# Diagonal spreads on GpSimd, state scaling on ScalarE, and unit 8's k turned through HBM, in a fused recurrence and MLP kernel

## The chip, the core and the metric

The kernel runs on one core of one Trainium2 chip. The metric is device time in microseconds (us) of one execution. Five engines run side by side, each through its own instructions in order: TensorE (PE), VectorE (DVE), ScalarE (ACT), GpSimd (POOL) and SyncE (SP, which only issues transfers here). Each waits on semaphores for what the others make.

## The reference

A linear recurrence over 768 time steps for 4 batches and 8 heads of 48 channels, and behind it a two-layer MLP with an ELU between (384 to 2048 to 384), all in float32:

```python
for t in range(S):
    cur = np.einsum('bhd,bhe->bhde', u[None] * kt, vt)
    y[:, :, t] = np.einsum('bhd,bhde->bhe', rt, state + cur)
    state = wt[:, :, :, None] * state + np.einsum('bhd,bhe->bhde', kt, vt)
...
h = x @ w_in
g = np.where(h > 0.0, h, alpha * (np.exp(np.minimum(h, 0.0)) - 1.0))
return (g @ w_out).astype(np.float32)
```

## The kernel before

**The recurrence in units.** The sequence is worked on in 24 units. Units 0 to 3 ("whole") are one batch each with 128 steps; units 4 to 23 hold two batches with 64 steps each. In a unit the recurrence is turned into products of matrices. Two scans on VectorE (es, L461, and gs, L471) make running products of the decay w; rh (L476) multiplies k and r by them. TensorE forms the scores of all pairs of steps in PSUM (task s: four transposes of k, L563, then score products, L570). A tile `ams` receives the diagonal (each step's own term, r times u times k summed over a head's channels, called md, spread over a matrix that is zero elsewhere: task sp) and then, by a predicated copy from PSUM on VectorE (mk, L599 to L605), the part above it. Task v multiplies `ams` with the values (L550) and updates the state (L640). Between units the state is scaled by the unit's total decay (sc, L632) and added to (up, L698).

**md** comes, in units 0 to 3, from VectorE (rkc, r times k, L495), TensorE (pd, L500) and a copy on ScalarE (L504); from unit 4 on from three VectorE steps (rk, rku, md). **sp** is run for units 0 to 7 by ScalarE, as eight scaled copies of the identity (L518), and for units 8 to 23 by GpSimd, as two selects on 64 partitions (L529).

**From unit 8 on** (`STACK`) r and the state are copied by DMA beside the scores and the values (rc, L540, and tc, L546), and the scores of the next unit are made one unit ahead (va). k with time on the partitions comes for units 9 to 21 (`TURN`) from a 32 by 32 transpose on VectorE (tn, L618), four transfers to HBM (tw, L623) and one back (tk, L627); for the others from transposes on TensorE (tr) and a copy on ScalarE (kt, L609).

**The MLP.** Each group of four units gives 512 columns, and 16 blocks of 128 hidden channels are run over them. float32 is split into a high and a low part (fp32r), so that g1 (`ph`, L267) and g2 (`acc`, L298) are nine matmuls each. Between them stand r1 and r2 on ScalarE (L271, L274), stt on VectorE (L277, written back to `m`), gh on ScalarE (L281) and gl on VectorE (L285). `ph` has two buffers, so a g1 waits for the stt of the g1 two before it. The weights are made at the start from raw words: a (ScalarE, L231), cc (VectorE, L235), wh (ScalarE, and for two blocks GpSimd, L727), wl (VectorE, L731).

**What sets the order.** The order on every engine is written out by hand as a table of names (`SEQUENCE`), one row per engine; a name is a task and its number, such as `sp.4`. `FILL` puts matmuls on a tile of ones (L426) ahead of named TensorE tasks before the first g2; they compute nothing that is used. One such float32 matmul shows as two records in the trace. Transfers are issued in order on SP's queue, and tiles with a fixed number of buffers (`SLOTS`) make a task wait for the last use of its buffer.

## Time and profile before

| | us |
|---|---|
| median of 3 runs (484.72 to 485.08) | 484.99 |
| the profiled execution | 486.13 |
| its span, first to last instruction | 484.4 |
| TensorE busy | 475.7 |
| VectorE busy | 359.1 |
| ScalarE busy | 260.4 |
| GpSimd busy | 40.7 |

The span is what the profile shows. The profiled execution took 1.73 us more than its span, and 1.14 us more than the median of the runs without a profile. Matmuls overlap in the engine and their ends are modelled, so the time that a matmul costs is read from one start to the next. The granted TensorE clock is 1.00 in every stretch of the trace.

### The profile page before, as it was taken

Reading aid. Unit: us, or ns where it says so; the run is one execution under the profiler, and the core shown is the slowest. Engines: PE = TensorE matmul, PEld = TensorE weight load, DVE = VectorE, ACT = ScalarE, POOL = GpSimd, SP = SyncE. Lnnn points to the kernel's source line nnn. Section 1 sums busy time; section 2 is a strip of 40 time slices with the busy share of each in tenths; the row PEclk is TensorE's granted clock in tenths of the full one; section 3 lists DMA queues with packets and bytes.
Section 4 is the critical chain, followed back from the end, with each engine's and each line's share of the span. In section 5 each row is a group of like instructions: output and inputs, shape, how many; then the busy total and the mean of one; then the engine's idle time right before and its main releaser. Section 6 shows DMA issues by size and latency. Waiting matters only on the chain.

```text
span 484.4 us, 12143 instructions
## 1 busy us (share of the span) xinstructions
PE 475.7 (98%) x4978; PEld 395.3 (82%) x4978; DVE 359.1 (74%) x545; ACT 260.4 (54%) x535; POOL 40.7 (8%) x56
## 2 busy tenths in 40 slices
PE   9999999999999999999999999999999999999996
PEld 8888888878888787788788878888888888888885
DVE  7999999999899999979997896655426453333332
ACT  4998878856544443635343643536544343644442
POOL 3000000004011302012101101101001000000000
PEclk9999999999999999999999999999999999999999
DMA  8999477417485664855754747332521100100001
GB/s 276 363 319 293 149 250 244 146 41 205 89 260 129 187 141 117 241 146 104 209 156 107 216 101 207 89 87 81 133 59 39 38 2 1 65 2 0 0 2 66
DMA packets 75418, 64.91 MB, mean 134 GB/s; under 512 B 56976, under 2 KB 57360, under 8 KB 75360
## 3 DMA queue, kind: packets, MB, share of 16 engines
q1 hardware_dynamic: 74784, 63.33, 46.3%
q8 instruction: 39, 0.64, 0.6%
q10 hardware_dynamic: 576, 0.79, 0.5%
q14 instruction: 19, 0.16, 0.1%
HBM read 49.67 MB, written 8.13 MB: 119 GB/s over the span
## 4 chain that ended last, share of the span: by engine, by line
PE 75%; DVE 16%; issue 3%; DMA 3%; ACT 2%; DVEq 0%; POOL 0%; POOLq 0%
PE ph L267 32%; PE acc L298 31%; PE py L550 2%; PE px L570 2%; PE acc L426 2%; DVE ams L605 2%; DVE m L277 2%; PE px L550 2%; DVE gl L285 2%; DVE eg L461 2%; DMA w<-in_wkr_dram 1%; DVE k L476 1%; PE px L640 1%; DVE tops L734 1%; DMA k<-in_wkr_dram 1%
## 5 line engine op out<-in xcount | busy, mean ns | idle before, releaser
L271 ACT ACTIVATE m<-ph 128x512 f32<-128x512 f32 (+2 forms) x103 | 58.3, 567 | 102.0 <-PE ph L267 69.8
L267 PE MATMUL ph<-xh,w_l 128*128 128x512 f32 (+1 forms) x294 | 112.0, 381 | 0.0
L298 PE MATMUL acc<-gh,w_l 128*128 128x512 f32 (+1 forms) x292 | 111.2, 381 | 0.0
L277 DVE SCALAR_TENSOR_TENSOR m<-m,ph 128x512 f32<-128x512 f32 (+2 forms) x103 | 66.2, 646 | 57.2 <-ACT m L274 56.6
L281 ACT CAST gh<-m 128x512 fp32r<-128x512 f32 (+1 forms) x98 | 58.9, 602 | 86.6 <-PE acc L298 60.4
L267 PE MATMUL ph<-xh,w_h 128*128 128x512 f32 (+1 forms) x264 | 102.5, 388 | 1.8 <-DVE m L277 1.4
L298 PE MATMUL acc<-gh,w_h 128*128 128x512 f32 (+1 forms) x264 | 102.3, 388 | 0.0
L285 DVE TENSOR_TENSOR gl<-m,gh 128x512 fp32r<-128x512 f32 (+1 forms) x98 | 67.0, 690 | 46.3 <-ACT gh L281 45.1
L298 PE MATMUL acc<-gl,w_h 128*128 128x512 f32 (+1 forms) x264 | 100.4, 380 | 0.3 <-DVE gl L285 0.3
L267 PE MATMUL ph<-xl,w_h 128*128 128x512 f32 (+1 forms) x264 | 100.3, 380 | 0.0
L267 PEld LDWEIGHTS ph<-xh,w_l 128*128 128x128 f32 x294 | 55.3, 188 | 10.8
L298 PEld LDWEIGHTS acc<-gh,w_l 128*128 128x128 f32 x292 | 54.9, 188 | 10.5
L274 ACT ACTIVATE m<-m 128x512 f32<-128x512 f32 (+2 forms) x103 | 61.2, 601 | 1.7
L267 PEld LDWEIGHTS ph<-xh,w_h 128*128 128x128 f32 x264 | 49.6, 188 | 13.8 <-DVE m L277 3.3
L298 PEld LDWEIGHTS acc<-gh,w_h 128*128 128x128 f32 x264 | 49.6, 188 | 10.3
L298 PEld LDWEIGHTS acc<-gl,w_h 128*128 128x128 f32 x264 | 49.6, 188 | 9.7 <-DVE gl L285 0.7
L267 PEld LDWEIGHTS ph<-xl,w_h 128*128 128x128 f32 x264 | 49.7, 188 | 8.9
L529 POOL TENSOR_SCALAR_AFFINE_SELECT ams<-md 64x512 f32<-64x512 f32 x32 | 32.1, 1002 | 242.2 <-PE py L550 164.2
L461 DVE TENSOR_TENSOR_SCAN eg<-w,reset 112x520 f32<-112x520 f32 (+1 forms) x24 | 30.1, 1256 | 2.8 <-DMA w<-in_wkr_dram 2.8
L471 DVE TENSOR_TENSOR_SCAN eg<-w,reset 112x520 f32<-112x520 f32 (+1 forms) x24 | 30.3, 1263 | 0.8
L476 DVE TENSOR_TENSOR k<-k,eg 112x1024 f32<-112x1024 f32 x24 | 29.1, 1214 | 0.1
L605 DVE COPY_PREDICATED ams<-upper_h,px 64x512 f32<-64x512 uint32 x32 | 23.5, 735 | 1.4 <-PE px L570 0.9
(127 smaller groups left out, 501.6 us busy)
## 6 DMA issues: line engine op xcount, KB each, us to landing
wraw<-in_wraw_dram SPq DMA_DIRECT2D x16, 767.8 KB, 6.6
rk<-in_rk_dram SPq DMA_DIRECT2D x20, 384.0 KB, 4.5
k<-in_wkr_dram SPq DMA_DIRECT2D x13, 512.0 KB, 4.3
w<-in_wkr_dram SPq DMA_DIRECT2D x24, 227.9 KB, 4.1
k<-in_wkr_dram SPq DMA_DIRECT2D x11, 448.0 KB, 5.5
wide<-in_vp_dram SPq DMA_DIRECT2D x32, 128.0 KB, 4.0
out_dram<-o SPq DMA_DIRECT2D x15, 256.0 KB, 4.0
rows<-turn SPq DMA_DIRECT2D x52, 64.0 KB, 2.8
```

Of the source, the lines that this page charges most:

```text
L267: nc.tensor.matmul(ph, w[f][:, 0, k], y[:, k], start=(k == n == 0), stop=(k == NK - 1 and n == 2))
L271: act(s["m"], s["ph"], AF.Relu, scale=-1.0)
L274: act(s["m"], s["m"], AF.Exp, scale=-1.0)
L277: stt_(s["m"], s["m"], -1.0, s["ph"], ALU.add, ALU.max)
L281: nc.scalar.copy(s["gh"], s["m"])
L285: nc.vector.tensor_tensor(s["gl"], s["m"], s["gh"].bitcast(F32), ALU.subtract)
L298: nc.tensor.matmul(a_, w[f][:, 1, m], fold(s, g[:, a:b]), start=(first and n == 0), stop=(final and n == 2))
L461: nc.vector.tensor_tensor_scan(out=eg[:, 0, 0:n][:, ::-1], data0=u_["w"][:, 1:n + 1][:, ::-1], data1=reset[:, 0, 0:n][:, ::-1], initial=0. ...
L471: nc.vector.tensor_tensor_scan(out=u_["eg"][:, 1, 1:n + 1], data0=u_["w"][:, 0:n], data1=reset[:, 1, 0:n], initial=0.0, op0=ALU.mult, op1= ...
L476: tt(t, t, u_["eg"][:, :, 0:u_["n"]].rearrange("d z (s t) -> d z s t", t=u_["L"] + 1)[..., 1:], ALU.mult)
L529: nc.gpsimd.affine_select(out=am[rs, h].rearrange("t q p s -> t (q p) s"), in_=u_["md"][rs].rearrange("t q p -> t (q p)").unsqueeze(2).bro ...
L605: nc.vector.copy_predicated(u_["am"][rs, h], above[L][rs], pa[rs])
```

## The change

Four things change, and with them the whole order.

- **Spreads.** sp of units 0 to 7 goes from ScalarE to GpSimd (`spread_rows`): one select of 128 partitions by 1024 elements for units 0 to 3, two of 64 by 512 for units 4 to 7.
- **Scaling.** sc of units 4 to 11 goes from one VectorE instruction to eight scaled copies on ScalarE (`scale_state_act`), each of 112 partitions by 48 elements. Units 12 to 23 stay.
- **Unit 8's k** is turned as that of units 9 to 21: tn.8 on VectorE, tw.8 and tk.8 through HBM. tr.8 on TensorE and kt.8 on ScalarE go.
- **pd** writes in the order that md is read in, at two places of its bank by turns, behind the place of the transposes; it no longer waits for the bank.
- **Sequences and fillers** are new for all engines. The fillers before the first g2 are 45 instead of 36.

```diff
-FILL = {("pd",0):17,("s",0):5,("pd",1):3,("s",1):2,("v",1):8,("s",2):1,("g2",0):0}
+FILL = {("s",0):23,("s",1):5,("v",0):2,("g1",0):4,("v",1):7,("g1",1):4,("g2",0):0}
...
-SPREAD = ["ACT"] * 8 + ["POOL"] * 16
+SPREAD = ['ROWS'] * 8 + ['POOL'] * 16
+SCALE = ['ACT' if i < 12 else 'DVE' for i in range(NU)]
-TURN = range(9, 22)
+TURN = range(8, 22)
...
     PE="""
-pd.0 s.0 pd.1 v.0 s.1 g1.0 pd.2 v.1 g1.1 g1.2 s.2 g2.0 g2.1 g1.3 pd.3 g2.2 v.2 g1.4 s.3 g2.3 g1.5 v.3 g1.6 g1.7 g2.4 g1.8 g2.5 g2.6 g1.9 g2.7 g2.8
+s.0 pd.0 pd.1 s.1 v.0 g1.0 v.1 g1.1 g1.2 g2.0 g2.1 pd.2 s.2 g1.3 g1.4 v.2 pd.3 g2.2 s.3 g2.3 g1.5 v.3 g1.6 g2.4 g1.7 g1.8 g2.5 g2.6 g1.9 g2.7 g1.10
...
     POOL="""
-const reset.4 clear.0 clear.1 clear.2 sp.9 sp.8 sp.10 sp.11 sp.12 wh.1 wh.0 sp.13 sp.14 sp.15 sp.16 sp.17 sp.18 sp.19 sp.20 sp.21 sp.22 sp.23
+const sp.0 sp.1 sp.2 reset.4 sp.3 clear.0 sp.4 sp.5 sp.6 clear.1 sp.7 sp.8 clear.2 sp.9 wh.1 sp.10 wh.0 sp.11 sp.12 sp.13 sp.14 sp.15 sp.16 sp.17
+sp.18 sp.19 sp.20 sp.21 sp.22 sp.23
...
     def diag_pe(u_):
-        u_["pd"] = pd = single()[:, 0:NS].rearrange("t (p z) -> t p z", p=NP)
+        lo = NP * R2 + NS * (u_["i"] % 2)
+        u_["pd"] = pd = single()[:, lo:lo + NS].rearrange("t (z p) -> t z p", p=NP)
         for p in range(NP):
-            nc.tensor.matmul(pd[:, p], u_["rkc"][:, p, :], ubd[:, p, :], start=True, stop=True)
+            nc.tensor.matmul(pd[:, :, p], u_["rkc"][:, p, :], ubd[:, p, :], start=True, stop=True)
...
-    def spread_act(u_):
-        am = diagonal(u_)
-        for q in range(2):
-            for p in range(NP):
-                act(am[:, q, p], ident if u_["whole"] else ident_h, AF.Copy, scale=u_["md"][:, q, p:p + 1])
...
+    def spread_rows(u_):
+        am, n = diagonal(u_).rearrange("t q p s -> t (q p) s"), u_["L"]
+        for lo in range(0, C, n):
+            rs = slice(lo, lo + n)
+            nc.gpsimd.affine_select(out=am[rs], in_=u_["md"][rs].rearrange("t q p -> t (q p)").unsqueeze(2).broadcast_to([n, NS, n]),
+                                    pattern=[[0, NS], [1, n]], compare_op=ALU.is_equal, fill=0.0, base=0, channel_multiplier=-1)
...
+    def scale_state_act(u_):
+        lo = u_["b"].start
+        for p in range(NP):
+            for h in range(2):
+                act(sv[:, lo + h, p], sv[:, lo + h, p], AF.Copy, scale=u_["pc"][:, 2 * p + h])
...
-            add(("s", i), "PE", K["s0" if u_["whole"] else "s8" if new else "s"], lambda u_=u_: score(u_),
-                [("rh", i), ("const",)] + [("sp", i)] * (i > 1) + before * (not new))
+                [("rh", i), ("const",)] + before * (not new))
...
-            hold("pb", ("pd", i), [("md", i)], fifo=False)
+            hold("pd", ("pd", i), [("md", i)])
```

TensorE at the start of the program, before and then after. `acc<-ones` are fillers, `py<-ident,k` and `px<-k` task s, `py<-ubd,rkc` pd, `ams,wide` and `wide,kt` v, `wide,w_f` the first g1.

```order
L426 MATMUL acc<-ones 128x128 x17
L500 MATMUL py<-ubd,rkc 128x2 x4
L426 MATMUL acc<-ones 128x128 x5
L563 MATMUL py<-ident,k 128x112 x4
L570 MATMUL px<-k 128x128 x8
L426 MATMUL acc<-ones 128x128 x3
L500 MATMUL py<-ubd,rkc 128x2 x4
L550 MATMUL px<-ams,wide 32x128 x16
L640 MATMUL px<-wide,kt 48x48 x8
```

```order
L428 MATMUL acc<-ones 128x128 x23
L563 MATMUL py<-ident,k 128x112 x4
L570 MATMUL px<-k 128x128 x8
L503 MATMUL py<-ubd,rkc 128x2 x8
L428 MATMUL acc<-ones 128x128 x5
L563 MATMUL py<-ident,k 128x112 x4
L570 MATMUL acc<-k 128x128 x8
L428 MATMUL acc<-ones 128x128 x2
L550 MATMUL px<-ams,wide 32x128 x16
L646 MATMUL px<-wide,kt 48x48 x8
L428 MATMUL acc<-ones 128x128 x4
L265 MATMUL ph<-wide,w_f 128x128 x3
```

The first scores now come before the first diagonal products, both of which stand together, and the scores of unit 1 come before the values of unit 0.

VectorE at the same place, before and then after; `eg<-w` are the scans, `rkc<-k` is rkc, `k<-k,eg` is rh, `w_f<-wraw` is cc and `ams<-upper` is mk.

```order
L461 SCALAR_TENSOR_TENSOR eg<-w,reset 112x516
L470 RECIPROCAL reset<-eg 112x4
L471 SCALAR_TENSOR_TENSOR eg<-w,reset 112x516
L495 TENSOR_TENSOR rkc<-k 112x512
L461 SCALAR_TENSOR_TENSOR eg<-w,reset 112x516
L476 TENSOR_TENSOR k<-k,eg 112x1024
L470 RECIPROCAL reset<-eg 112x4
L471 SCALAR_TENSOR_TENSOR eg<-w,reset 112x516
L495 TENSOR_TENSOR rkc<-k 112x512
L599 COPY_PREDICATED ams<-upper,px 128x512 x2
```

```order
L463 SCALAR_TENSOR_TENSOR eg<-w,reset 112x516
L472 RECIPROCAL reset<-eg 112x4
L473 SCALAR_TENSOR_TENSOR eg<-w,reset 112x516
L497 TENSOR_TENSOR rkc<-k 112x512
L478 TENSOR_TENSOR k<-k,eg 112x1024
L463 SCALAR_TENSOR_TENSOR eg<-w,reset 112x516
L497 TENSOR_TENSOR rkc<-k 112x512
L472 RECIPROCAL reset<-eg 112x4
L473 SCALAR_TENSOR_TENSOR eg<-w,reset 112x516
L478 TENSOR_TENSOR k<-k,eg 112x1024
L237 SCALAR_TENSOR_TENSOR w_f<-wraw,top 128x768
L599 COPY_PREDICATED ams<-upper,px 128x512 x2
```

rh of unit 0 moves ahead of the second unit's first scan, and mk of unit 0 behind rh of unit 1 and the first cc.

GpSimd behind its constants, before and then after; `ams<-md` are the spreads, `wide` the clearing of tiles for unit 8 and on, `w_g<-wt` the casts of two weight blocks.

```order
L387 MEMSET reset 112x1040
L388 MEMSET reset 112x8
L535 MEMSET wide 32x512 x3
L529 AFFINE_SELECT ams<-md 64x512 x10
L727 CAST w_g<-wt 128x768 x2
L529 AFFINE_SELECT ams<-md 64x512 x22
```

```order
L522 AFFINE_SELECT ams<-md 128x1024 x3
L389 MEMSET reset 112x1040
L390 MEMSET reset 112x8
L522 AFFINE_SELECT ams<-md 128x1024
L535 MEMSET wide 32x512
L522 AFFINE_SELECT ams<-md 64x512 x6
L535 MEMSET wide 32x512
L522 AFFINE_SELECT ams<-md 64x512 x2
L529 AFFINE_SELECT ams<-md 64x512 x2
L535 MEMSET wide 32x512
L529 AFFINE_SELECT ams<-md 64x512 x2
L733 CAST w_g<-wt 128x768
```

The reset tile for unit 4 and the clearings now stand between spreads on GpSimd, and the two casts are apart.

## Rows read from the trace of the kernel before

**Rows 1.** The page, busy time of each engine in us, its share and count.
```profile
PE 475.7 (98%) x4978; PEld 395.3 (82%) x4978; DVE 359.1 (74%) x545; ACT 260.4 (54%) x535; POOL 40.7 (8%) x56
```

**Rows 2.** Two stretches: length, busy us (instructions) of PE, PEld, DVE, ACT, POOL; granted clock; DMA.
```profile
20.00:30.00 10.00, 9.79 (x117) 8.86 (x116) 9.96 (x17) 9.18 (x23) 1.08 (x2) 1.00 0.83 288
...
160.00:200.00 40.00, 38.73 (x405) 31.02 (x404) 38.25 (x57) 19.52 (x42) 8.20 (x8) 1.00 0.64 160
```

**Rows 3.** TensorE in order of time, first 41 us: start, length, what, idle before.
```profile
1.08 6.61 PE L426 MATMUL acc<-ones 128*128 128x128 f32 x34 [1.08 <-POOL ones L391]
7.53 0.95 PE L500 MATMUL py<-ubd,rkc 112*128 112x2 f32 x8
...
18.14 2.03 PE L426 MATMUL acc<-ones 128*128 128x128 f32 x16
20.10 1.08 PE L550 MATMUL acc<-ams,wide 128*32 128x128 f32 x32
...
35.53 0.39 PE L298 MATMUL acc<-gl,w_h 128*128 128x256 f32 x1 [0.28 <-DVE gl L285]
...
37.54 0.28 PE L267 MATMUL ph<-xh,w_l 128*128 128x256 f32 x1
38.54 1.08 PE L550 MATMUL px<-ams,wide 128*32 128x128 f32 x32 [0.72 <-DVE ams L599]
...
40.04 0.39 PE L267 MATMUL ph<-xh,w_h 128*128 128x256 f32 x1
```

**Rows 4.** VectorE and one load on SP's queue in order of time, first 10 us.
```profile
1.75 0.43 SPq L429 DMA_DIRECT2D ubd<-in_uz_dram  x1
...
3.87 1.23 DVE L461 TENSOR_TENSOR_SCAN eg<-w,reset 112x516 f32<-112x516 f32 x1 [1.40 <-DMA w<-in_wkr_dram]
...
7.08 1.23 DVE L461 TENSOR_TENSOR_SCAN eg<-w,reset 112x516 f32<-112x516 f32 x1
8.22 1.20 DVE L476 TENSOR_TENSOR k<-k,eg 112x1024 f32<-112x1024 f32 x1
```

**Rows 5.** TensorE's waits: who for whom, us in total, times, longest.
```profile
PE ph L267 <- DVE m L277: 1.4, 2, 1.0
...
PE px L550 <- issue: 1.0, 1, 1.0
...
PE ph L267 <- DVE reset L470: 0.2, 1, 0.2
```

**Rows 6.** VectorE's groups by shape: count, busy us, mean ns, idle before.
```profile
L285 DVE TENSOR_TENSOR gl<-m,gh 128x512 fp32r<-128x512 f32 x90 | 63.9, 714 | 46.3 <-ACT gh L281 45.1
...
L632 DVE TENSOR_TENSOR st<-st,pcs 112x384 f32<-112x384 f32 x20 | 11.0, 550 | 0.1
...
L618 DVE STREAM_TRANSPOSE turn<-k 128x512 f32<-128x512 f32 x13 | 9.1, 702 | 0.0
```

**Rows 7.** ScalarE's and GpSimd's spreads by shape, the same columns.
```profile
L518 ACT ACTIVATE ams<-ident_h,md 128x64 f32<-128x64 f32 x32 | 8.0, 333 | 0.1
...
L529 POOL TENSOR_SCALAR_AFFINE_SELECT ams<-md 64x512 f32<-64x512 f32 x32 | 32.1, 1002 | 242.2 <-PE py L550 164.2 <-DVE md L490 64.4 <-DVE reset L470 12.6
```

**Rows 8.** GpSimd and VectorE side by side, in order of time.
```profile
117.49 0.69 DVE L285 TENSOR_TENSOR gl<-m,gh 128x512 fp32r<-128x512 f32 x1 [0.76 <-ACT gh L281]
...
162.70 1.33 DVE L285 TENSOR_TENSOR gl<-m,gh 128x512 fp32r<-128x512 f32 x1 [0.74 <-ACT gh L281]
...
206.26 2.19 POOL L529 TENSOR_SCALAR_AFFINE_SELECT ams<-md 64x512 f32<-64x512 f32 x2 [12.57 <-DVE reset L470]
...
206.28 1.72 DVE L471 TENSOR_TENSOR_SCAN eg<-w,reset 112x520 f32<-112x520 f32 x1
```

**Rows 9.** Unit 8's transposes on TensorE, in order of time.
```profile
116.15 0.55 PE L563 MATMUL py<-ident,k 112*128 112x112 f32 x4
```

**Rows 10.** DMA issues of the turned k: count, KB each, us to landing.
```profile
rows<-turn SPq DMA_DIRECT2D x52, 64.0 KB, 2.8
turn<-rows SPq DMA_DIRECT2D x13, 256.0 KB, 4.2
```

146 lines of the change are left out of this document (70 added, 76 removed).

## Prediction

> **What bounds the kernel now.** I read the busy times first: TensorE is busy for 475.7 of 484.4 us and VectorE for 359.1 [rows 1]. TensorE's share says little by itself, since its fillers count as busy too. So I read the stretches next. From 20 to 30 us VectorE works 9.96 of 10 us and ScalarE 9.18, and from 160 to 200 us VectorE still 38.25 of 40, while ScalarE is down to 19.52 [rows 2]. So for the first 200 us VectorE runs beside TensorE with almost nothing to spare. Third, TensorE's own order of time. Its first product that is used starts at 7.53 us; 34 filler records stand before it, and by `FILL` 38 more follow (19 fillers, two records each); the value products of unit 3 start at 38.54 us, and the MLP runs on from 40.04 us [rows 3]. Last, its waits: behind that point the view lists 1.4 us behind VectorE's stt in two waits, 0.2 us behind VectorE's reciprocal, and 1.0 us with no cause that the profile shows [rows 5]: 1.6 us behind VectorE, 2.6 us in all. From 40 us on the kernel is TensorE's matmuls one behind the other plus these 2.6 us and smaller gaps. A change can win by a shorter front, by fewer matmuls, or by taking these waits away.
>
> **The front, up to the first product behind unit 3's values.** By the orders, the same tasks stand before that point in both kernels: all s, pd and v of units 0 to 3, g1 to number 5 and g2 to number 3. So I compare the fillers, the start and the waits.
> - The start. One filler record costs 1.96 / 16 = 0.12 us (18.14 to 20.10 us) [rows 3]. The first used product now stands behind 23 fillers, 46 records: 34 of them took until 7.53 us, 12 more add 1.47, so 9.0 us. Its input is rh of unit 0. That stood behind another scan, which starts at 7.08 us, where rh would now stand; the small load of `ubd` now goes first on SP's queue and puts the w load back by one issue, 0.43 us; rh takes 1.20 us [rows 4]. That gives 8.71 us, so the fillers decide: +1.47 us.
> - Fillers behind the start: 22, that is 44 records instead of 38: +0.74 us. Seven of them stand in front of unit 1's values, which VectorE has ready earlier than before, as both rkc, both rh and only one cc precede its mk; there is nothing to take their place, so they lie on the path.
> - Waits. Two of before are in this stretch: 0.28 us at 35.53, and 38.54 less 37.54 less 0.12, 0.88 us, before unit 3's values [rows 3]. VectorE has less to do now up to unit 3's mk (two scans, of units 4 and 5, stand behind it instead of ahead, for one maximum that stands ahead), so I let both go: -1.16 us.
> The front comes to +1.47 + 0.74 - 1.16 = **+1.05 us**. Its ends: +0.3 if smaller gaps go as well; +2.05 if GpSimd's spreads come late (below).
>
> **Unit 8's transposes.** tr.8 leaves TensorE: 0.55 us [rows 9], on the path, since nothing fills its place: **-0.55 us**. What it moves: kt.8 leaves ScalarE, tn.8 adds 0.70 us to VectorE [rows 6], and five issues go into SP's queue. The turned k needs 2.8 + 4.2 = 7.0 us of landing [rows 10]. In the new VectorE order 21 tasks stand between tn.8 and unit 8's mask; at VectorE's mean of 359.1 / 545 = 0.66 us [rows 1] that is 14 us, so the 7 us are hidden; but tk.8 is queued behind rc.8, which waits for GpSimd's spread of unit 8, and the loads behind it would wait with it. If that cover were gone, unit 8's values and the update that unit 10 needs would be late by what is missing.
>
> **VectorE's relief, and what GpSimd takes of it.** Eight sc leave VectorE: 8 x 0.55 = 4.4 us [rows 6]; tn.8 adds 0.70. Neighbours overlap by some 0.09 us (7.08 to 8.22 is 1.14 for an instruction of 1.23 [rows 4]), so the relief is 4.4 - 0.7 - 7 x 0.09 = 3.1 us, in units 4 to 11, where VectorE is full.
> Against it stand the spreads. The trace shows GpSimd and VectorE in each other's way. A scan takes 1.23 us by itself [rows 4] and 1.72 us while a spread runs; a gl takes 0.69 us, and 1.33 us while GpSimd's cast runs [rows 8]. The spreads' own mean is 1.00 us [rows 7]. So one spread of 64 by 512 can cost VectorE 0.49 us. The change adds eight of those, and four with twice the elements in a partition, which no row shows; taken as two each, the upper bound is 16 x 0.49 = 7.8 us, and the lower one is nothing, since VectorE also has steps that a spread does not touch. Over the run gl lost 90 x (0.714 - 0.69) = 2.2 us [rows 6] to 32 spreads and two casts, some 0.07 each, and the scans have a like share; I take 0.1 us for each of the 16, 1.6 us in all, as these rows are of the same kind of work. Net relief: 3.1 - 1.6 = 1.5 us, about the 1.6 us that TensorE waits behind VectorE. I let 1.35 of these go and keep 0.25.
>
> **Beside other work, at nothing.** ScalarE gives up eight spreads; the four half ones took 8.0 us, 0.25 us a copy [rows 7]. It takes on eight scalings of eight copies, each with 48 elements instead of 64: at most 64 x 0.25 = 16 us, where the eight spreads gave back 16 us or more. It is at 54% [rows 1]. The cover is that a scaling stands in ScalarE's order where up of the unit before is done; were it not, r1, r2 and gh queue behind it, and TensorE behind those. On GpSimd the reset for unit 4 and the clearings now stand between spreads; the second clearing waits for unit 6's values, and between md and the mask of unit 7 VectorE has three steps of some 2.3 us for a spread of 2.0 [rows 7], the tightest place of the eight. pd's second place costs nothing. At the end one copy of the last sums now stands behind another on ScalarE and still beside TensorE's last products.
>
> **The wait with no cause.** 1.0 us inside one value product [rows 5]. Nothing in the change touches it, but every instruction before it moves. Half: -0.5 us (ends 0 and -1.0).
>
> **The sum.** 484.4 + 1.05 - 0.55 - 1.35 - 0.5 = 483.05 us of span. The profiled execution was 1.73 us longer than its span and 1.14 us longer than the median of the runs; both stay, so 486.13 - 1.35 = 484.78 there and 484.99 - 1.35 = **483.6 us** as the median. A measurement of this kernel can tell about 0.2% from no change: 484.0 to 486.0 is the same.
>
> **Rivals.**
> - A, slower: GpSimd takes the whole relief. Spreads 0 and 2 become ready just when VectorE has nothing but steps of two SBUF operands before its mask; the mask then waits for the spread, 1.0 us each, half of which TensorE sees: front +2.05. In units 4 to 7 each of the eight spreads costs its full 0.49 us, 3.9 us, more than the relief of 3.1, and all waits stay: 484.4 + 2.05 - 0.55 = 485.9, so **486.5**. It decides once a spread costs VectorE 0.2 us in the mean. For it: the rows of 206 us. Against: the mean of gl.
>  The Trainium skill has a rule that speaks for A (SBUF — State Buffer, "Who interferes with whom"): a VectorE instruction with two SBUF inputs and a GpSimd instruction that reads SBUF share a read interface, and the second to start blocks until the first has finished. The 1.72 us scan agrees with it; by the rule every meeting costs a whole instruction, which is A's price.
> - B, the same: the waits come back elsewhere. The new order is as tight as the old, and what VectorE gains it spends on doing other steps earlier; only the wait with no cause is halved: 484.4 + 1.05 - 0.55 - 0.5 = 484.4, so **485.0**. For it: VectorE at 96% even from 160 to 200 us.
> - C, everything goes: front +0.3, and all 2.6 us: 484.4 + 0.3 - 0.55 - 2.6 = 481.55, so **482.1**, and 481.5 with small gaps.
> - D, the change does not do what it says: unit 8's k is not there in time, and TensorE waits some 3 us before unit 8's values: 483.6 + 3 = **486.6**.
>
> **How the numbers follow.** My forecast has 0.44 (its own range 482.4 to 484.3), B 0.25, A 0.17, C 0.08, D 0.06. Faster: C and nearly all of the forecast, 0.50. The same: B and the forecast's upper edge, 0.27. Slower: A and D, 0.23. The range that leaves 2 in 10 out goes from 481.5 to 486.6 us.
>
> **What would show it.** TensorE's first used product near 9.0 us, and the first matmul behind unit 3's values near 41.1 us. No transposes of unit 8 on TensorE. Eight 48-element copies on ScalarE at 0.25 us or less. Spreads on 128 partitions of 1 to 2.5 us. TensorE's waits behind VectorE below 0.5 us in the view. Scans and gl with a mean as before: if they are longer by 0.05 us or more, A holds. I am wrong in the front if the masks of units 0 and 2 wait for GpSimd, and wrong in the rest if the waits of the view still come to 2 us or more.

## The result

| | before | after |
|---|---|---|
| median of six runs, us | 484.96 | 490.12 |
| lowest and highest | 484.72 to 485.10 | 487.59 to 491.27 |
| profiled execution | 486.13 | 488.53 |
| its span | 484.4 | 486.8 |

The changed kernel is slower: by the ratio of the runs its time is 1.0098 times that of before (95% interval 1.0074 to 1.0121). I had forecast 483.6 us and a range to 486.6. Of all runs below, one of 1201 us and one of 1383 us count as slow and are in no median, range or ratio here.

TensorE's own order of time tells where the time went (columns as in [rows 3]; "front" is the stretch up to the first product behind unit 3's values, "rest" what follows):

```profile
9.37 0.58 PE L563 MATMUL py<-ident,k 112*128 112x112 f32 x4
9.87 1.16 PE L570 MATMUL px<-k 48*128 48x128 f32 x16
10.96 1.05 PE L503 MATMUL py<-ubd,rkc 112*128 112x2 f32 x8
12.64 1.05 PE L503 MATMUL py<-ubd,rkc 112*128 112x2 f32 x8 [0.62 <-ACT kt L609]
13.55 1.97 PE L428 MATMUL acc<-ones 128*128 128x128 f32 x10
15.32 0.95 PE L563 MATMUL py<-ident,k 112*128 112x112 f32 x4
16.20 1.77 PE L570 MATMUL acc<-k 48*128 48x128 f32 x16
17.91 0.71 PE L428 MATMUL acc<-ones 128*128 128x128 f32 x4
18.55 1.08 PE L550 MATMUL px<-ams,wide 128*32 128x128 f32 x32
...
29.18 0.95 PE L503 MATMUL py<-ubd,rkc 112*128 112x2 f32 x8
31.24 0.57 PE L563 MATMUL py<-ident,k 112*128 112x112 f32 x4 [1.10 <-ACT md L516]
...
35.78 1.08 PE L550 MATMUL px<-ams,wide 128*32 128x128 f32 x32 [0.53 <-issue]
...
43.49 1.08 PE L550 MATMUL px<-ams,wide 128*32 128x128 f32 x32
...
45.00 0.39 PE L269 MATMUL ph<-xh,w_h 128*128 128x256 f32 x1
```

The last two rows, the values of unit 3 and the first product behind them, answer to 38.54 and 40.04 us in [rows 3]. The front is **4.96 us longer**, where I had +1.05. From unit 3's values to TensorE's last product the changed kernel takes 439.3 us, before 442.2: **2.9 us less**, where I had 2.4 less. Of these 2.9 us, 1.0 is the stop without a cause of [rows 5], which this profile of after does not have. The two profiles differ by 2.40 us: 4.95 of front, less 2.88, and 0.33 behind the last product. The medians differ by 5.16, since the profiled execution of before lay 1.17 us above its median and that of after 1.59 below.

TensorE's waits of after (columns as in [rows 5]). Those of [rows 5], 2.6 us in all, are gone. Others stand in their place; all but the second row lie in the front:

```profile
PE py L563 <- ACT md L516: 1.1, 1, 1.1
...
PE acc L300 <- DVE gl L287: 0.8, 2, 0.5
PE py L503 <- ACT kt L609: 0.6, 1, 0.6
PE px L550 <- issue: 0.5, 1, 0.5
```

The granted clock is the second thing to see. Stretches of after: length, busy us (instructions) of PE, PEld, DVE, ACT, POOL; granted clock; DMA.

```profile
10.00:14.00 4.00, 3.38 (x36) 3.17 (x37) 3.54 (x5) 0.90 (x4) 0.04 (x1) 1.00 1.04 357
14.00:17.50 3.50, 3.50 (x25) 3.22 (x25) 2.60 (x4) 2.32 (x4) 2.82 (x2) 0.52 1.03 406
17.50:20.00 2.50, 2.50 (x60) 2.06 (x58) 2.38 (x4) 0.00 (x0) 0.00 (x0) 0.99 1.03 298
...
160.00:200.00 40.00, 39.99 (x531) 32.51 (x530) 39.65 (x61) 20.76 (x47) 6.15 (x6) 1.00 0.68 173
```

From 14 to 17.5 us TensorE ran at the lower of its two levels, 1.2 GHz, behind the diagonal products of two columns (8 matmuls, 16 records) and the stop of 0.62 us; before has no such stretch. Unit 1's transposes and scores took 2.59 us there (15.32 to 17.91), against 1.57 before (14.99 to 16.56):

```profile
14.99 0.55 PE L563 MATMUL py<-ident,k 112*128 112x112 f32 x4
15.47 1.16 PE L570 MATMUL acc<-k 48*128 48x128 f32 x16
16.56 0.94 PE L263 MATMUL ph<-wide,w_f 128*128 128x128 f32 x6
```

From 160 to 200 us TensorE is now busy for 39.99 of 40 us, where [rows 2] had 38.73: the wait at 165 us is gone. In the six runs the mean granted clock went from 0.995 (spans of 485.8 and 486.8 us) down to 0.987 (489.5): the spread of the runs goes with the clock.

One reading of the time before has to be put right here: that its clock is 1.00 in every stretch. The trace's record of the granted clock begins at 6.5 us in before and at 7.3 us in after, with the upper level; for the time ahead of it the view prints 1.00 without a record. At that moment the fillers go from 0.21 to 0.11 us apart, start to start. Fillers at a recorded 1.2 GHz are also 0.21 us apart (14.25 to 15.1 us in after), and at 2.4 GHz 0.11. So by their pitch the first fillers ran at the lower level, and the record begins with the clock's first rise.

Why the stops are there shows on the other engines (ScalarE, VectorE, GpSimd of after, the same columns; `m<-ph` is r1, `m<-m,ph` stt and `k<-k,eg` rh):

```profile
12.05 0.53 ACT L609 COPY kt<-py 128x448 f32<-128x448 f32 x1 [9.95 <-PE py L503]
...
13.73 0.17 ACT L516 COPY md<-py 128x8 f32<-128x8 f32 x1 [1.05 <-PE py L503]
...
28.71 0.38 ACT L273 ACTIVATE m<-ph 128x256 f32<-128x256 f32 x1 [1.34 <-PE acc L297]
...
30.69 0.15 ACT L516 COPY md<-py 128x8 f32<-128x8 f32 x1
```
```profile
4.71 1.23 DVE L463 TENSOR_TENSOR_SCAN eg<-w,reset 112x516 f32<-112x516 f32 x1 [2.24 <-DMA w<-in_wkr_dram]
...
8.04 1.23 DVE L478 TENSOR_TENSOR k<-k,eg 112x1024 f32<-112x1024 f32 x1
...
29.58 0.42 DVE L279 SCALAR_TENSOR_TENSOR m<-m,ph 128x256 f32<-128x256 f32 x1 [1.21 <-ACT m L276]
29.92 1.22 DVE L478 TENSOR_TENSOR k<-k,eg 112x1024 f32<-112x1024 f32 x1
31.05 0.95 DVE L737 TENSOR_TENSOR w_l<-wg,w_h 128x768 fp32r<-128x768 f32 x1
31.92 0.55 DVE L696 TENSOR_TENSOR xl<-wide,xh 128x384 fp32r<-128x384 f32 x1
32.39 0.95 DVE L237 SCALAR_TENSOR_TENSOR wg<-wraw,top 128x768 uint32<-128x768 uint32 x1
34.33 1.35 DVE L599 COPY_PREDICATED ams<-upper,px 128x512 f32<-128x512 uint32 x2 [0.99 <-POOL ams L522]
```
```profile
30.91 3.39 POOL L522 TENSOR_SCALAR_AFFINE_SELECT ams<-md 128x1024 f32<-128x1024 f32 x1 [14.09 <-ACT md L516]
```

**Units 0 and 1.** Unit 0's transposes and both units' diagonal products share the PSUM tile `py`, and the kernel lets a copy out of it and products into it follow one another. The copy of the turned k waits until unit 0's diagonal products are through (12.05), unit 1's products wait for that copy, and the copy of unit 0's diagonal waits for unit 1's products (13.73), though its own were ready at 12.0. So pd still waits for its bank, which the change was to end.

The Trainium skill (PSUM — Partial Sum Buffer, "Terms") says why a program keeps such accesses apart: two engines at once on one bank and the same 32 partitions are an error. No run here lets them meet; the waits at 12.05, 12.64 and 13.73 us are what keeping them apart costs in this order.

**Unit 2.** At 28.71 ScalarE's r1 waits for the g2 that frees its buffer (g2 0); r2, VectorE's stt (29.58) and behind it unit 2's rh (29.92 to 31.14) follow one another. TensorE's load for the transposes starts at 31.21, 0.07 us behind the end of rh. The view names the copy of unit 2's diagonal for this wait, but that was over at 30.84. In all seven profiles with the new front the load starts 0.07 us behind rh, whenever the copy ended.

Spread 2 then starts into VectorE's steps on SBUF operands and takes 3.39 us; mask 2 waits 0.99 us for it. The mask ends at 35.68 and unit 2's values start at 35.78, behind the wait of 0.53 us for which the view names nothing.

The groups of after that answer to [rows 6, 7]:

```profile
L287 DVE TENSOR_TENSOR gl<-m,gh 128x512 fp32r<-128x512 f32 x90 | 62.1, 693 | 43.2 <-ACT gh L283 42.5
...
L473 DVE TENSOR_TENSOR_SCAN eg<-w,reset 112x520 f32<-112x520 f32 x20 | 26.2, 1310 | 0.7
...
L638 ACT ACTIVATE st<-st,pcs 112x48 f32<-112x48 f32 x64 | 15.3, 323 | 0.7 <-DVE st L704 0.7
L522 POOL TENSOR_SCALAR_AFFINE_SELECT ams<-md 64x512 f32<-64x512 f32 x8 | 11.3, 1418 | 35.3 <-DVE md L492 35.0
...
L522 POOL TENSOR_SCALAR_AFFINE_SELECT ams<-md 128x1024 f32<-128x1024 f32 x4 | 7.5, 1888 | 23.2 <-ACT md L516 23.2
```

### The profile page after: what moved, and what is told of

Its sections match the earlier page's. It is cut to its first block, busy times and chain, and to the rows that moved or that the text cites. A ratio compares the mean times of both kernels' runs of the same rounds, so it can differ in the third digit from the quotient of the medians.

```text
span 486.8 us, 12170 instructions
## 1 busy us (share of the span) xinstructions
PE 478.6 (98%) x4992; PEld 398.7 (82%) x4992; DVE 355.5 (73%) x538; ACT 257.9 (53%) x534; POOL 58.0 (12%) x68
## 4 chain that ended last, share of the span: by engine, by line
PE 83%; DVE 12%; issue 3%; POOL 1%; ACT 1%; DVEq 0%; POOLq 0%
PE acc L300 34%; PE ph L269 34%; PE py L550 3%; PE acc L428 3%; PE px L570 3%; DVE gl L287 2%; DVE eg L463 1%; DVE m L279 1%; PE px L646 1%; DVE k L478 1%; PE ph L265 1%; PE px L550 1%; PE acc L297 1%; DVE ams L605 1%; DVE w_l L737 1%
## 5 line engine op out<-in xcount | busy, mean ns | idle before, releaser
L287 DVE TENSOR_TENSOR gl<-m,gh 128x512 fp32r<-128x512 f32 (+1 forms) x98 | 65.3, 670 | 43.2 <-ACT gh L283 42.5
L529 POOL TENSOR_SCALAR_AFFINE_SELECT ams<-md 64x512 f32<-64x512 f32 x32 | 29.7, 928 | 216.5 <-PE py L550 136.9
L522 POOL TENSOR_SCALAR_AFFINE_SELECT ams<-md 64x512 f32<-64x512 f32 (+1 forms) x12 | 18.9, 1575 | 58.5 <-DVE md L492 35.0
```

The costliest lines, as they stand in the source:

```text
L287: nc.vector.tensor_tensor(s["gl"], s["m"], s["gh"].bitcast(F32), ALU.subtract)
L529: nc.gpsimd.affine_select(out=am[rs, h].rearrange("t q p s -> t (q p) s"), in_=u_["md"][rs].rearrange("t q p -> t (q p)").unsqueeze(2).bro ...
```

## The experiments

Ratios are to the kernel before in the same series, with 95% intervals. Where a version is called the kernel before with a part of the change, or with the old front, it has the code of pd from the changed kernel too; unit 3's values start at 38.3 to 38.7 us in those that move nothing else ahead of them, as in before.

### Which half: the old front with the new rest

```diff
-FILL = {("s",0):23,("s",1):5, ...}       # and the new SEQUENCE up to unit 3's values
+FILL = {("pd",0):17,("s",0):5, ...}      # both as before the change
-SPREAD = ['ROWS'] * 8 + ['POOL'] * 16
+SPREAD = ['ACT'] * 4 + ['ROWS'] * 4 + ['POOL'] * 16
```


> The changed kernel with the kernel before's order and fillers up to unit 3's values (up to mask 3 on VectorE, turned k of unit 3 on ScalarE, the seventh MLP weight's load on SP), and spreads 0 to 3 on ScalarE; behind that point everything as in the changed kernel. Theory front: the trace of the changed kernel reaches the first matmul behind unit 3's values 5.0 us later (45.00 instead of 40.04 us) and takes 2.6 us less from there to the end, because transposes and waits are gone there; both are independent, so this kernel comes to 485.0 - 2.6 = 482.4 us and is the faster of all three. Rival slack: the rest is shorter only because a TensorE that is 5 us late finds VectorE, ScalarE and the loads ahead of it; with the old front the waits return, only unit 8's transposes (0.55 us) stay away, and the time is 484.4 us.

Measured: 485.22 us (483.79 to 487.84), ratio 1.0003 (0.9985 to 1.0021). The profile took 484.52 us: unit 3's values at 38.70, and 439.85 us from there to the last product, 2.3 less than before. So the front is what makes the change slow, 4.6 us by the ratios and 4.9 by the medians. Rival slack is wrong on the rest, which is shorter without a late TensorE too; the wait of 1.0 us behind stt at 165 us has not come back. But the time, 485.2, is nearer to the rival's 484.4 than to my 482.4: the median gained nothing, so half of the theory fell too. Two repeats for a second profile of each:

> The kernel before, unchanged, for a second profile. In the first one (486.13 us, 1.14 above the median) TensorE stops for 1.2 us inside unit 7's state products at 104.3 us, with no cause shown. Theory: that stop belongs to single executions; the spans of the other runs lie at 483.1 to 483.6 and at 484.2 to 484.6 us, two groups 1.1 us apart. If this profile's span is near 483.3 it does not have the stop, and if it is near 484.4 it has. Then the gain of the rest is to be counted from 483.3, not from 484.4. Rival: the stop is there at either span; then the groups have another cause.

> The kernel with the old front, unchanged, for a second profile. Its spans lay between 481.9 and 485.9 us; the first profile (482.5 us) was one of the short ones. Theory: what makes the longer ones longer are single stops of TensorE of 0.8 to 1.5 us without a cause in the profile, as in before, and falls of the clock in the front; a profile of 483.5 us or more shows at least one of them, a profile near 482 us none. Rival: the longer ones wait for unit 8's turned k or for the spreads of GpSimd, and the view of the waits names them.

Measured: before 485.87 (span of the profile 484.2), the old front 486.04 (483.8), ratio 1.0015 (1.0000 to 1.0031). TensorE's waits, the row with no cause, of before_again and old_front_again:

```profile
PE px L550 <- issue: 0.7, 1, 0.7
```
```profile
PE px L556 <- issue: 1.5, 1, 1.5
```

It is the same place as in [rows 5], unit 7's state products, where TensorE stands still until 105.4 and 104.7 us. Eight of the twenty profiles of this study have this stop, of 0.7 to 1.5 us, the others have none. The old front shows it with and without: its first profile has no stop and a span of 482.5 us, the second a stop of 1.5 and 483.8. The spans of before fall in two groups, 482.9 to 483.6 and 483.9 to 484.9; both of its profiles are of the upper one and show the stop, none of the lower was profiled. That the stop is what parts the groups of before is therefore likely and not shown. If it is, the gain of the rest against a run without it is 2.3 less 1.0, about 1.3 us; the lowest spans, 481.9 and 482.9, are 1.0 apart. Of the 22 runs with the old front five have a mean clock of 0.995 or 0.996 and spans of 485.3 to 486.3; of the runs of before beside them, none. What brings the clock down in those five no profile caught: open.

### The clock in the front

Six edits of the changed kernel, each to its front alone.

```diff
-FILL = {("s",0):23,("s",1):5, ...}
+FILL = {("s",0):23,("pd",1):5, ...}                   # fill_pd1
+FILL = {("s",0):23,("pd",1):4,("s",1):5, ...}         # cover_pd1
+FILL = {("s",0):31,("pd",1):4,("s",1):5, ...}         # start_cover
```


> The changed kernel with five fillers (ten records) moved from in front of unit 1's scores to in front of unit 1's diagonal products, into the place where TensorE stood still for 0.62 us (12.0 to 12.64 us) between sixteen two-column products; nothing else moves. Theory clock: that stop brought the granted clock down to the 1.2 GHz level from 14.1 to 17.4 us, where unit 1's transposes and scores took 2.58 us instead of 1.57 and ten fillers 1.77 instead of 1.2. Without it the granted clock from 10 to 20 us is 1.00, the front is 1.2 to 1.6 us shorter, so about 488.7 us, and the runs lie closer together than 487.6 to 491.3. Rival: the low clock has another cause (or only fills a wait that stays), the fillers only push unit 1's diagonal back by 0.3 us: 490.1 to 490.5 us, and the same spread of runs.

Measured: 491.00 us (488.68 to 493.40). Wrong: the moved fillers left a stop where they had stood (TensorE idle from 14.0 to 15.25 us, until the copy of unit 1's diagonal out of `py` ended at 15.18), and the clock was low from 15.9 to 22.7 us.

> The changed kernel with four more fillers (eight records, 0.9 us at the higher clock) in front of unit 1's diagonal products, where TensorE stood still from 12.0 to 12.64 us; the five in front of unit 1's scores stay where they are, so this kernel only has more to do. Theory clock: in the four profiles of the changed front each fall to the 1.2 GHz level (from 14.1, 15.5, 16.1 and 12.1 us, for 3.4 to 10.7 us) came behind a stop of TensorE between 11.4 and 15.3 us, and the kernel before, without such a stop there, has no fall. With the stop covered there is no fall before 20 us, unit 1's transposes and scores take 1.6 us, and the time falls by 1.2 to 2 us to 488 to 489 us, although work was added. Rival: the sixteen two-column products themselves, or unit 1's inputs that come late, bring the clock down: then the fall stays (from 14 to 16 us on), and the time is 490.1 to 491 us.

Measured: 491.34 us (490.28 to 494.51). Wrong again, and its profile shows why (the first row is cut off by a window that starts at 6 us):

```profile
5.82 2.29 PE L428 MATMUL acc<-ones 128*128 128x128 f32 x19
9.23 0.57 PE L563 MATMUL py<-ident,k 112*128 112x112 f32 x4 [1.13 <-issue]
```
```profile
11.00:24.80 13.80, 13.80 (x107) 12.51 (x108) 7.95 (x9) 3.37 (x8) 2.85 (x2) 0.51 1.03 331
```

The clock's first rise, and with it the step from 0.21 to 0.11 us between fillers, came at 7.3 us in the profile of after and at 4.5 us here; it moves from one execution to the next (4.0 to 7.3 us in the twenty profiles). Here it came early, the 46th record started at 7.8 instead of 9.15 us, TensorE stood until 9.23, and the clock fell at 11.3 us. (The list of this version has an entry `("s",2):6` too; that task stands behind the first g2, and no filler comes of it: 98 records in all, 90 in after.)

> As the run with four fillers more in front of unit 1's diagonal products, and eight more (31 instead of 23) in front of the first used product. In the trace of that run the clock had risen early, the 46 filler records were through at 7.9 us, TensorE stood still for 1.3 us until unit 0's rows were there (9.2 us), and the clock fell at 11.1 us for 13.5 us. Theory stops: each early fall comes from a stop of TensorE, at the start or behind the first diagonal products; with both covered the granted clock is 1.00 from 5 to 30 us, and the time is 487 to 489 us, though twelve fillers (2.7 us at the higher clock) were added. Rival two-column: the sixteen diagonal products, two columns each, bring the clock down whatever stands beside them: a fall before 20 us remains, 490 to 493 us.

Measured: 489.78 us (488.91 to 490.49), ratio 1.0088 (1.0074 to 1.0103). Its profile has 1.00 from 10 to 32.0 us, with the same two-column products: they alone do not bring the clock down, and rival two-column is wrong. Each of the five early falls (at 11.3 to 16.3 us) had a stop of 0.5 to 1.2 us shortly before it. But a stop alone does not decide either: three profiles with the old order of the front stand 0.60 to 0.76 us just before their first product (6.5 to 7.4 us) and have no fall. Here the stop of 1.1 us before unit 2's transposes (until 30.45 us) had a fall behind it, at 32.0 us; in after the same stop (1.10 us) had none. What decides there is open. Unit 3's values start at 43.56 us, in after at 43.49: twelve fillers cost what the clock gave back.

```diff
-s.0 pd.0 pd.1 s.1 v.0        # TensorE; ScalarE: md.1 behind kt.1; 31 and 7 fillers ahead of s.0 and s.1
+s.0 pd.0 s.1 pd.1 v.0
```


> The changed kernel with unit 1's diagonal products behind unit 1's scores instead of ahead of them (and their copy behind unit 1's turned k on ScalarE), with 31 fillers in front of the first used product and seven instead of five in front of unit 1's scores. Theory order: unit 0's diagonal is copied out at 12.7 us instead of 13.73, since nothing is written to its PSUM bank ahead of it, so conversion, spread and mask 0 come 1 us or more earlier, unit 0's values start near 16.5 us instead of 18.55, and the two-column products no longer stand back to back, so there is no fall of the clock before 20 us: 486 to 488 us. Rival: unit 1's mask is now late by what unit 0's gained (its spread starts near 18 instead of 15 us), unit 1's values start no earlier than 23.4 us, and the time is that of the run that only adds fillers.

Measured: 489.85 us (488.11 to 491.03), ratio 1.0088. No fall in its profile (the other runs have mean clocks of 0.994 to 1.000), and unit 3's values start at 42.98 us: 4.4 us later than before, and only 0.5 us earlier than in after, with fillers until 10.8 us and the stop of 1.1 us before unit 2's transposes (until 30.72). So with the clock at its upper level the new front is nearly as long. The clock is one of two prices for the same thing, a TensorE that has nothing ready; the other is the fillers. The span of this profile, 489.3 us, is no measure of its front: the rest took 1.2 us more than in after, and 5.8 us instead of 4.0 passed behind TensorE's last product (5.5 in the profile of start_cover, 3.7 to 4.2 in all others). The cause of that is open.

```diff
-kt.0 pc.0 md.0 a.0           # ScalarE, with the fillers of fill_pd1
+md.0 kt.0 pc.0 a.0           # and SLOTS pd=1: unit 1's products wait for this copy
```


> The kernel with the moved fillers, and in addition unit 0's diagonal is copied out (ScalarE) ahead of its turned k, and before unit 1's diagonal products are written. In the changed kernel this copy is ready at 12.0 us and starts at 13.73, since it waits for the products of unit 1 in the same PSUM bank; the weight conversion behind it and VectorE's step behind that wait too (VectorE idle 1.29 us before 14.90). Theory order: the copy starts 1.5 us earlier, spread 0 and mask 0 follow, unit 0's values start 1 to 1.5 us earlier than with the fillers alone, and the time falls by as much (about 487.5 us if the fillers alone give 488.7). Rival: unit 1's scan and product on VectorE, not the copy, set when unit 0's values and unit 1's scores can start; the time stays as with the fillers alone.

Measured: 488.07 us (486.74 to 490.55), 2.9 less than fill_pd1, of the same series, and 1.6 (by the ratios) to 2.0 less than the changed kernel. Unit 0's values start at 16.77 us instead of 18.85, unit 3's at 43.02 instead of 45.52. The theory holds as to the way, but the shared tile by itself is worth less than that: from unit 1's diagonal products to its transposes TensorE takes 1.49 us instead of 2.20, 0.7 us less. Some 1.6 of the 2.5 us at unit 3's values lie in transposes, scores and fillers that ran at the lower clock in fill_pd1; here the clock was low for 3.5 us instead of 6.8. That the shorter stop (0.5 instead of 1.2 us) is why it was low for less is likely and not shown.

```diff
-g2.0 g2.1 pd.2 s.2           # TensorE; ScalarE: md.2 moved ahead of wh.3
+pd.2 g2.0 g2.1 s.2
```


> The changed kernel with unit 2's diagonal products two MLP groups earlier on TensorE (ahead of g2.0 and g2.1) and their copy two steps earlier on ScalarE (ahead of wh.3 and xh.1); the fillers as in the changed kernel. There unit 2's transposes wait 1.10 us for this copy (31.24 us), and unit 2's values 0.53 us for a mask that waits for GpSimd's spread (3.39 us long beside VectorE's steps). Theory order: the first wait goes, and the second becomes shorter, since the spread starts before VectorE's steps with two SBUF operands: 1.1 to 1.6 us less than the changed kernel, 488.5 to 489.0 us. Rival port: the spread still meets those steps and the mask still waits for it, so what the transposes win the values lose again: 0 to 0.5 us less. The clock theory adds nothing here: the low clock before 20 us stays.

Measured: 493.16 us (492.82 to 495.92), 3 us slower instead of 1.4 faster. ScalarE, VectorE and TensorE in this profile:

```profile
32.66 0.38 ACT L273 ACTIVATE m<-ph 128x256 f32<-128x256 f32 x1 [2.86 <-PE acc L297]
```
```profile
33.87 1.92 DVE L478 TENSOR_TENSOR k<-k,eg 112x1024 f32<-112x1024 f32 x1
```
```profile
35.88 0.66 PE L563 MATMUL py<-ident,k 112*128 112x112 f32 x4 [2.59 <-ACT top L233]
```

g2.0 frees the buffer for which r1 waits. Moved behind pd.2 it came later, r1 waited 2.86 instead of 1.34 us, and unit 2's rh on VectorE stood behind its stt. The copy of the diagonal now ended at 33.55 us, yet the transposes waited for rh, until 35.79: the stop of 1.10 us became 2.59, with a second fall of the clock (36.2 to 43.1 us). rh itself took 1.92 instead of 1.22 us, as the spread, now earlier, ran beside it (33.62 to 34.71). The view names ScalarE's step a, which ended at 35.75. In after I had taken the view's releaser for the cause, and had not looked at what the products I put back release.

### The place of the spreads and scalings

```diff
-SPREAD = ['ACT'] * 4 + ['ROWS'] * 4 + ...    # the kernel with the old front
+SPREAD = ['ROWS'] * 8 + ...                  # POOL: const sp.0 sp.1 sp.2 reset.4 sp.3 ...
```


> The kernel with the old front, but spreads 0 to 3 on GpSimd as in the change (one of 128 by 1024 each) instead of 32 copies on ScalarE (8 copies of 0.33 us for each spread). It tells whether the place of the spreads or the new order makes the changed front 5 us longer. Theory order: GpSimd is as good a place; ScalarE is freed of 10 us, TensorE reaches the first matmul behind unit 3's values between 38 and 40.5 us (40.2 in the run with the old front), and the time is 484 to 485.5 us. Rival A, GpSimd's port: spreads of 2 to 3.4 us beside VectorE's steps of two SBUF operands; the masks of units 0 to 3 wait for them, VectorE stands 1 us or more before at least two of them, and the time rises by 1 to 4 us.

Measured: 487.27 us (485.82 to 489.18), ratio 1.0045 (1.0030 to 1.0059), 2.05 us more than the first series of the old front and 1.2 more than the second; unit 3's values start 1.95 us later (40.65). Rival A's price, but not at the masks: none in the front waits for a spread. GpSimd and VectorE of this profile, two pairs:

```profile
8.93 1.62 POOL L528 TENSOR_SCALAR_AFFINE_SELECT ams<-md 128x1024 f32<-128x1024 f32 x1 [4.09 <-ACT md L516]
13.66 2.73 POOL L528 TENSOR_SCALAR_AFFINE_SELECT ams<-md 128x1024 f32<-128x1024 f32 x1 [3.11 <-ACT md L516]
```
```profile
9.73 1.91 DVE L473 TENSOR_TENSOR_SCAN eg<-w,reset 112x516 f32<-112x516 f32 x1
...
15.36 2.12 DVE L463 TENSOR_TENSOR_SCAN eg<-w,reset 112x516 f32<-112x516 f32 x1
```

The same scans take 1.23 and 1.22 us with the spreads on ScalarE. Of the two engines the one that comes second loses: here the scan, 0.7 to 0.9 us; in the changed front spread 2 (3.39 us). The rule of the Trainium skill that I cited for A (SBUF — State Buffer, "Who interferes with whom") describes this. These rows agree with it: the two spreads end at 10.55 and 16.39 us, and a scan that waited for that and then took its 1.23 or 1.22 us would end at 11.78 and 17.61; they end at 11.64 and 17.48.

```diff
-SPREAD = ['ACT'] * 8 + ['POOL'] * 16         # the kernel before, its SEQUENCE otherwise
+SPREAD = ['ACT'] * 4 + ['ROWS'] * 4 + ['POOL'] * 16
-(no SCALE: sc on VectorE)
+SCALE = ['ACT' if i < 12 else 'DVE' ...]     # scale_spread only; sc.4 to sc.7 in the places of sp.4 to sp.7
```


> The kernel before with one part of the change: GpSimd spreads diagonals 4 to 7 (two of 64 by 512 each), and ScalarE is rid of them (8 us) without anything in their place; spreads 0 to 3 stay on ScalarE, the scalings on VectorE. By my sum the contention costs VectorE 0.1 us for each of the eight, 0.8 us, of which TensorE sees at most half, and ScalarE's relief gives something back: 484.7 to 485.4 us. Rival A: each spread costs VectorE its 0.49 us, 3.9 us in all, and TensorE's waits behind VectorE between 50 and 110 us grow by 2 us or more: 487 us.

> As the run with spreads 4 to 7 on GpSimd, and the scalings of units 4 to 11 on ScalarE instead of VectorE (eight copies each, 0.32 us a copy in the changed kernel's trace), in the places of the four spreads and behind the updates that they need. By my sum VectorE gains 8 x 0.55 less overlap, 3.7 us, and TensorE's 1.6 us of waits behind VectorE fall to 0.3: 1.3 us faster than with the spreads alone, 483.4 to 484.1 us. Rival: VectorE only does other steps earlier, the waits were set by the order, not by VectorE's load, and the time stays within 0.3 us of the spreads alone; or ScalarE's longer block (2.2 to 2.6 us) holds up r1, r2 and gh, and TensorE waits behind ScalarE or gl instead: slower by up to 1 us.

Measured: the spreads alone 486.63 us, ratio 1.0020 (1.0006 to 1.0034), a cost of 1.0 us, between my sum and rival A; with the scalings 486.03 us, ratio 1.0013 (1.0002 to 1.0025). VectorE of spread_alone beside spread 4 (47.23 to 49.20) and spread 5 (56.32 to 59.43):

```profile
47.41 1.28 DVE L237 SCALAR_TENSOR_TENSOR wg<-wraw,top 128x768 uint32<-128x768 uint32 x1
48.61 1.40 DVE L743 TENSOR_TENSOR w_l<-wg,w_h 128x768 fp32r<-128x768 f32 x1
...
56.50 1.54 DVE L478 TENSOR_TENSOR k<-k,eg 112x1024 f32<-112x1024 f32 x1
```

Before, the three took 0.96, 0.95 and 1.22 us: 1.09 us lost, and unit 4's values start 0.9 us later (60.16 instead of 59.27). The scalings then give 0.35 us by the ratios and 0.6 by the medians; the lowest spans of both are 484.1, so the relief of 3.1 us was worth little. The wait behind stt at 165 us, which I had put down to VectorE's load, is still there with the scalings moved, and longer (1.4 us, before 1.0): the old order sets it. Together the two parts cost 0.6 us in the old order.

### Unit 8's k, and the order

```diff
-TURN = range(9, 22)          # the kernel before; tr.8 and kt.8 out, tn.8 behind rh.8
+TURN = range(8, 22)          # SP: ld_rk.11 tw.8 tw.9 tk.8 (turn8_alone); tw.8 ld_rk.10 ..., tn.9 later (turn8_cover)
```


> The kernel before with one part of the change: unit 8's k goes by VectorE and HBM, so its transposes leave TensorE and the copy leaves ScalarE; nothing else moves. By my sum: -0.55 us, 484.4 to 484.7 us. Rival D: unit 8's turned k or what is queued behind it on SP is late, TensorE waits before unit 8's values: 0 to +3 us and a wait in front of them in the trace. Third: VectorE, which is full at that place, pays 0.7 us for the turn and gives the 0.55 us back as a wait behind stt or gl: 485.0 us.

Measured: 491.32 us (491.09 to 492.37). VectorE, then TensorE:

```profile
119.41 0.71 DVE L623 STREAM_TRANSPOSE turn<-k 128x512 f32<-128x512 f32 x1 [4.80 <-DMA rows<-turn]
```
```profile
123.41 0.79 PE L268 MATMUL ph<-xh,w_h 128*128 128x512 f32 x1 [4.42 <-DVE m L278]
```

I had put unit 8's transfers behind a load that waited 2.1 us for VectorE's md. Unit 9's turn waited for the one buffer, TensorE stopped for 4.4 us, and the clock was low from about 121 to 128 us. It is rival D's mechanism, made by my placement: in the changed order nothing waits there.

> The kernel before with unit 8's k through VectorE and HBM alone, as in the earlier run, but with the transfers ahead of the load of unit 10's r and k on SP's queue, and unit 9's turn three VectorE steps later. In the earlier run they were queued behind a load that waited for VectorE, unit 9's turn stood 4.8 us before the buffer was free, TensorE stopped for 4.6 us at 118.6 us, and the clock fell. Theory: with that cover the part is worth its term, -0.55 us: 484.4 to 484.7 us against 485.0. Rival: VectorE pays 0.7 us for the turn where it is full, and a wait behind it gives the 0.55 us back: 484.9 to 485.5 us.

Measured: 487.77 us, ratio 1.0040 (1.0024 to 1.0055): slower even so. Its profile has a wait of 1.1 us behind stt (until 143.5 us) that before has not. So the rival is right in kind: VectorE pays, and more than the rival allowed.

```diff
-TURN = range(8, 22)          # the kernel with the old front; tn.8 tw.8 tk.8 out, tr.8 ahead of g2.22
+TURN = range(9, 22)          # kt.8 behind r2.23 (old_front_noturn), behind r2.24 (noturn_clean)
```


> The kernel with the old front, without the part on unit 8's k: unit 8's transposes are back on TensorE, its copy on ScalarE. The run with the old front has its median at that of the kernel before, but its runs lie between 483.8 and 487.8 us. Theory: the turned k is worth its 0.55 us, whatever else varies: 485.5 to 486 us, and the same spread of runs. Rival: its HBM route (nine transfers more near 110 us) is what makes some runs long; without it the runs lie within 1.5 us of each other and the median is 483.5 to 484.8 us.

Measured: 487.97 us, ratio 1.0060. No answer on the turn: kt.8, waiting for the transposes, and a scaling of 1.9 us stood ahead of gh.23 on ScalarE, VectorE's gl waited 2.8 us for it, and TensorE 1.7 us for VectorE's stt (until 123.1). So repeated with the copy further back:

> The kernel with the old front, without the part on unit 8's k, with the copy of the turned k behind gh.23 and r2.24 on ScalarE. Theory: the transposes are on TensorE's path and cost their 0.55 us again: 0.5 to 0.6 us more than with the old front, in the median and from unit 7's values to unit 8's. Rival: VectorE is full there and the turn that it is spared (0.70 us) gives the 0.55 us back: within 0.2 us of the old front, or below.

Measured: 484.54 us (483.88 to 487.56), ratio 0.9995 (0.9978 to 1.0011). From unit 7's values to unit 8's TensorE takes 22.07 us, with the turn 21.60: the transposes do cost 0.47 us there, but the time is not less with the turn. From unit 3's values to the last product it takes 439.7 us, with the turn 439.85. The rival holds.

```diff
-SPREAD = ['ACT'] * 4 + ['ROWS'] * 4 + ...; SCALE = ['ACT' if i < 12 ...]     # the kernel with the old front
+SPREAD = ['ACT'] * 8 + ...; SCALE = ['DVE'] * NU                             # sc.i behind rh.i or up
```


> The kernel with the old front and the new order behind it, but with spreads 4 to 7 on ScalarE and the scalings of units 4 to 11 on VectorE, as in the kernel before: what is left of the change is unit 8's turn and the order. Theory parts: the spreads on GpSimd cost 1.0 us and the scalings on ScalarE give 0.4 us back, so without both the time is 0.6 us less than with the old front: 484.4 to 484.8 us, less than either kernel. Rival: the new order was made for a VectorE and a ScalarE without these steps; with them the waits behind stt and gl return, and the time is 485.5 to 488 us.

Measured: 491.67 us, ratio 1.0141. The rival, and more: waits of 1.3 us each behind gh and kt and 1.4 behind gl. With the spreads and scalings put back in these places the new order is slow; another placement was not tried. What a part is worth in one order cannot be carried over to another.

### My waits before unit 3's values

```diff
-cc.4 es.4 es.5 gl.3 wl.4 cc.5 mk.3           # VectorE, the kernel with the old front
+cc.4 gl.3 wl.4 cc.5 mk.3 ... wl.5 es.4 ... rh.4 es.5
```


> The kernel with the old front, and on VectorE the scans of units 4 and 5 (1.14 us each) behind unit 3's mask, in the places that the changed kernel gives them, instead of ahead of gl 3 and that mask. Theory, from my sum: these scans are why TensorE waits 0.55 us for gl at 35 us and 0.87 us for mask 3 at 37.6 us; both waits go, unit 3's values start 1.2 to 1.4 us earlier, and the time is 1.2 us less than with the old front: 484.0 to 484.8 us, below the kernel before. Rival: what is moved back is missed later (unit 4's values wait for its rows), and the time stays within 0.4 us of the old front's.

Measured: 485.43 us (483.15 to 488.88), ratio 1.0006 (0.9983 to 1.0028). Unit 3's values start at 37.60 us, 1.1 us earlier than in the first profile with the old front. The two scans were worth 1.1 us at that point, as my sum had it, and nothing in the time, as the rival had it. Its quickest run, 483.15, is the shortest of all, but four of twelve have clocks of 0.995 or 0.996 and 486.7 to 488.9 us. No version beats the kernel before beyond the uncertainty.

## Why the prediction was wrong

- **Start, +1.47: measured +1.84.** I had the fillers decide, with rh of unit 0 through at 8.71 us. In after rh (8.04) ends at 9.27 and the last filler record starts at 9.15, so the two set the start together. The load of w was issued 0.46 us later, as I had it, but the scan behind it started 0.84 us later (4.71 for 3.87). I had counted on the time of one execution: in the profiles of this front the 46th record starts anywhere from 7.8 to 9.2 us, as the clock's first rise moves, and rh ends between 8.6 and 9.3.
- **Fillers, +0.74: right**, and 0.47 more, as some of them ran at the lower clock.
- **Waits, -1.16: the step that failed.** I compared "the fillers, the start and the waits", and took from the waits of before those that go. These two did go: 0.53 us less at the g2 of the wait for gl, and 0.80 less at the products before unit 3's values. But I followed no new wait through the new order. The shared `py` costs 0.90 us at the diagonal products of units 0 and 1, where I had written that pd's second place costs nothing. The chain from g2 over r1, r2 and stt to rh costs 1.16 at unit 2's transposes, and the spread before mask 2 costs 0.62 at unit 2's values. And I had no term for the clock, 1.01 us at unit 1's scores and 0.47 at the fillers. What is not named is 1.78 us less, 1.33 of it at the two waits and 0.28 at unit 1's values: 1.84 + 0.74 + 0.47 + 0.90 + 1.01 + 1.16 + 0.62 - 1.78 = 4.96.
- **The median stands another 1.6 us above this profile.** By their mean clocks, 0.987 to 0.993 in four of the six runs, the falls are longer there; none of these was profiled. That the kernel before never falls behind its first rise I had read off from a 1.00 in every stretch, and took it for granted in the new order too.
- **Unit 8's transposes, -0.55:** 0.47 at the place, nothing in the time.
- **Relief and contention, -1.35: mis-sized in its parts.** I took 0.1 us for each of 16 spreads, 1.6 us. Measured in the old order: 1.95 us at unit 3's values for the four of the front and 1.0 in the time for the eight of units 4 to 7, some 3 us in all, and 0.35 to 0.6 us back in the time for a relief that I had at 3.1. That is rival A in the size of the contention. By the means that I named it hardly shows: gl 693 ns, the second scan of 520 elements 1310 where it had 1269; a few steps lose much and most nothing.
- **The rest as a whole came out as forecast, by luck.** Without the stop it is 1.9 us shorter, as the two terms of 0.55 and 1.35 say. But the runs give neither term its size: the turn gave nothing in the time, and the spreads and scalings together cost 0.6 us in the old order. The waits behind VectorE went with the new order.
- **The wait with no cause, -0.5: wrong in kind.** I took half of it off a median that does not hold it: the profiled execution lay 1.14 us above the median, and the stop, 1.0 us, is most likely that difference.
- **Rivals.** None gave 490. A named the right engine, and 486.5 is a loss; its +2.05 for the front at the masks is close to the 1.95 us measured in the old order, but by another path, VectorE's scans: luck. In the changed front mask 2 waits for GpSimd, 0.99 us, as A says, and mask 0 does not. D did not happen.
- **Signs.** First product at 9.37, not 9.0; unit 3's point at 45.0, not 41.1; waits behind VectorE in the view 0.8 us, not below 0.5; spreads on 128 partitions 1.1 to 3.4 us, not up to 2.5. The scalings' copies start 0.23 us apart, and no transposes of unit 8 are left on TensorE, as said.

## What to carry over

Where a start is a chain over four engines, compare orders by following every handover, the PSUM tile and the buffer that a product frees included: equal work on the longest engine says nothing. For a wait, compare the end of the step that the view names with the start of the one that waited; if they are 0.3 us or more apart here, another step was the last. In this front the falls of TensorE's clock followed short stops, and a profile at 1.00 throughout did not say how near it was to one. Take a stop without a cause off the profile only together with what sets that profile apart from the median.
